# Eight more key rows kept on the chip between two attentions, and a second operand moved from PSUM to SBUF

## The chip, the core and the metric

The kernel runs on one core of a Trainium2 chip. The core has five engines with queues of their own: TensorE (PE, matrix products, here into PSUM), VectorE (DVE), ScalarE (ACT), GpSimd (POOL) and SyncE (SP, which here only issues transfers). Two memories are on the core, SBUF and PSUM, each with 128 partitions; the inputs lie in HBM and come into SBUF by DMA. The metric is the device time of one launch in microseconds (us), the median of some runs.

## What is computed

Two transformer layers' worth of decoding for one new token in a batch of two, in float32, with the weights of the one layer used twice:

```python
def _A_ref(x, k_cache, v_cache, wq, wo):
    B, Sq, D = x.shape            # 2, 1, 576
    H, Dh = 32, 128               # caches: [2, 32, 8192, 128]
    q = (x @ wq).reshape(B, Sq, H, Dh).transpose(0, 2, 1, 3)
    scores = jnp.einsum("bhqd,bhkd->bhqk", q, k_cache) * (Dh ** -0.5)
    p = _softmax(scores, axis=-1)
    o = jnp.einsum("bhqk,bhkd->bhqd", p, v_cache)
    return o.transpose(0, 2, 1, 3).reshape(B, Sq, H * Dh) @ wo
...
x = A_x
x = x + _A_ref(_layernorm(x), A_k_cache, A_v_cache, A_wq, A_wo)
x = x + _B_ref(_layernorm(x), B_w_gate, B_w_up, B_w_down)
x = x + _A_ref(_layernorm(x), A_k_cache, A_v_cache, A_wq, A_wo)
x = x + _B_ref(_layernorm(x), B_w_gate, B_w_up, B_w_down)
```

`_B_ref` is a gated feed-forward block (576 to 4608 and back, gelu times the second product). Each cache holds 2 x 32 x 8192 x 128 floats, 268 MB, and each attention reads both of them: that is nearly all of the traffic.

## The kernel before

**Items.** A head's keys lie over the partitions by rows. Item 0 to 59 are pairs of heads of one batch element (64 partitions to a head, 128 key rows to a partition, 8 parts of 16 rows, 8.39 MB for keys and as much for values); items 60 to 63 (`SINGLE`) are single heads (128 partitions, 64 rows, 4 parts of 16 rows, 4.19 MB). The first attention (layer 0) goes through items 0 to 63, the second (layer 1) from 63 down to 0.

**Held data.** SBUF is filled by one arena, the tile `space`. At the end of the first attention the keys of items 62 and 63 and the values of 61 to 63 stay where they are and are used again in the second. Of item 61's keys, part 3 is copied to PSUM (`kept`, line 643) and copied back in the second attention (line 686); its parts 0 to 2 are loaded again.

**Scores of one item.** For each part, `multiply` (line 637) multiplies key rows by q on VectorE (line 651). The broadcast q of an item, `qb[n]`, is a matrix product in the PSUM tile `bank` (`query`, line 591, written at line 599). In items of several parts at once that is all; in the first five items of the second attention (`waited`: 63, 62, 61, 60, 59) VectorE takes 12 of a part's 16 rows and GpSimd the other 4 (line 655). GpSimd reads q from `qs`, an SBUF copy that ScalarE makes once for an item (line 650). Then GpSimd adds the upper half of each product row to the lower (line 668) for 9 rows, ScalarE sums the other 7 rows whole (line 661), and VectorE sums the halved rows (line 671, `add_up`). The first and last part of item 63 (`at_once`) have 11 rows summed on VectorE and no halving on GpSimd. `peak`, `highest` and `softmax` make the weights, `values` (line 800) multiplies them with the value rows on TensorE, `gather`, `context` and `divide` finish the item.

**Order.** The schedule is written by hand: each engine runs its instructions in the order in which the code emits them. The loop over items (line 871) puts `add_up`, `peak`, `softmax` of the item before, `values` of one before that and `query` of the next one between the parts of an item. Accesses of the engines to one PSUM bank are kept in emitted order by waits, also where they touch different columns of it; `bank` holds `xps`, two slots for `qb` and unused columns, `bank2` holds small results (`po`, `smalls`, `share`).

**Transfers.** All loads are issued by SP in one order, planned at build time (`plan_first`, `plan_mlp`, `plan_second`). A load is issued once its place in `space` has been given back by the last reader (`done`). In the second attention the order is: q weights; keys of 61 (parts 0, 1, 2) and of 60; keys of 59 and values of 60 part by part, into places of the items that are being used up; keys of 58 in two halves; values of 59 in two halves; then keys 57, values 58, keys 56, values 57 and so on, 8.39 MB each.

**Places used by the change.** `same` (line 461) is a constant [128, 128] matrix for the layer norms; `osb` (line 812) a [128, 128] tile for `gather`; `S` (line 640) holds an item's scores; `prz` (line 444) four slots of softmax weights, of which `idle_products` (line 531) also reads the first 256 columns as something to multiply; `qs` shares its buffer with the layer norm's `xc`.

Of the kernel before, what the change touches and what calls it, by code (L numbers as in the profile page):

```python
# [15 lines left out]
P = 128  # L16
B = 2
# [24 lines left out]
RING = 5 * SLOT  # L42
END = RING + NPLACE * PLACE
HELD = 5
FOLD = 2


# [76 lines left out]
def decode_layers(ctx, tc, x_in, kc, vc, wq, wo, wg, wu, wd, out):  # L124
# [32 lines left out]
    def part_at(at, n):  # L157
        return space[:, at:at + n]
# [1 line left out]
    def part(at):  # L160
        return part_at(at, PART).rearrange("p (j d) -> p j d", d=DH)

    def load(at, n, src, lo, hi):

        t = part_at(at, (hi - lo) * PART).rearrange("p (j d) -> p j d", d=DH)
        nc.sync.dma_start(t, ITEMS[n].source(src)[:, lo * JC:hi * JC, :])

    def cache(key, src, n, slots=None, pieces=None):

# [25 lines left out]

        queue.append(make)

    def one(key, src, n, k, where):

        def make():  # L200
            at = arena.ring((key, k), PART) if where is None else arena.take((key, k), places[where[0]][where[1]], PART)
            if at is None:
                return False
            load(at, n, src, k, k + 1)
            ready.setdefault(key, {})[k] = part(at)
            return True

        queue.append(make)
# [154 lines left out]
    def plan_second():  # L363

        for k in range(4):
            of_half(1, k)
        half_rows(("wq", 1, NU - 1), wq, single[-1], None)
        for k in range(4):
            of_half(0, k)
        last = PAIRS - 1  # L370
        k63, v63, k62, v62 = ("k", 1, SINGLE[3]), ("v", 1, SINGLE[3]), ("k", 1, SINGLE[2]), ("v", 1, SINGLE[2])

        for k in range(3):
            one(("k", 1, SINGLE[1]), kc, SINGLE[1], k, None)
        for k in range(4):
            one(("k", 1, SINGLE[0]), kc, SINGLE[0], k, (k63, k - 1) if k else None)

        one(("k", 1, last), kc, last, 0, (k63, 3))
        turns = iter(range(1, 5)), iter(range(4))
        for kind in "vvvvkkkk":  # L380
            if kind == "k":
                k = next(turns[0])
                one(("k", 1, last), kc, last, k, (k62, k - 1))
            else:
                k = next(turns[1])
                one(("v", 1, SINGLE[0]), vc, SINGLE[0], k, (v63, k))
        for k in range(5, 8):
            one(("k", 1, last), kc, last, k, (v62, k - 5))
        half(("k", 1, last - 1), kc, last - 1, 0, 5)
        half(("k", 1, last - 1), kc, last - 1, 4, 4)  # L390
        half(("v", 1, last), vc, last, 0, 0)
        half(("v", 1, last), vc, last, 4, 1)
        for n in range(last - 2, -1, -1):
            cache(("k", 1, n), kc, n)
            cache(("v", 1, n + 1), vc, n + 1)
        cache(("v", 1, 0), vc, 0, None, (4, 2, 1, 1))
        for g in groups(1):
            out_rows(1, g)
# [56 lines left out]
    for i in range(2):  # L455
# [2 lines left out]
    strip = consts.tile([P, 4], F32, name="strip")  # L458
    nc.vector.reduce_sum(strip, ident.rearrange("p (c r) -> p c r", c=4), axis=AX.X)

    same = consts.tile([P, P], F32, name="same")
    nc.vector.tensor_copy(
        same.rearrange("p (m b) -> p m b", b=B), pick[:, 0:B].unsqueeze(1).to_broadcast([P, P // B, B])
    )

# [16 lines left out]
    share = bank2[:, 2 * GH + 2 * P:2 * GH + 2 * P + FOLD * JC]  # L484
    kept = psum1.tile([P, JC, DH], F32, name="kept")

    def small(p, n):

        smalls.append(smalls.pop(0))
        return smalls[0][0:p, 0:n]  # L490


    def norm(split=False, then=None):
        stats = work.tile([P, 6], F32, name="stats")
        nc.vector.bn_stats(stats, x)
        apart = work.tile([P, 4, 6], F32, name="apart")
        nc.vector.tensor_mul(
            apart, stats.unsqueeze(1).to_broadcast([P, 4, 6]), strip.unsqueeze(2).to_broadcast([P, 4, 6])
        )
        every4 = small(P, 4 * 6)  # L500
        nc.tensor.matmul(every4, same, apart.rearrange("p c t -> p (c t)"), start=True, stop=True)
        mv = work.tile([P, 2], F32, name="mv")
        nc.vector.bn_aggr(mv, every4)
        xc = once.tile([P, CW, 2], F32, name="xc", tag="xc")
        xr = x.rearrange("p (m r) -> p r m", r=NU)
        xs = xc.rearrange("p w s -> p (w s)")
        if split:
            xm = xs[:, :5 * 32].rearrange("p (u m e) -> p u m e", u=5, e=2)
            parts = [(xm[:, 0:4, :, e], xr[:, 5 * e:5 * e + 4, :], 0) for e in range(2)]
            parts += [(xm[:, 4, :, e], xr[:, 4, :], e) for e in range(2)]  # L510
            xs = xs[:, :5 * 32].rearrange("p (u q) -> p u q", u=5)
        else:
            parts = [(xc[:, :, s], x, s) for s in range(2)]
            xs = xs.rearrange("p (q u) -> p u q", u=NU)
        for to, of_x, s in parts:
            nc.vector.tensor_scalar(to, of_x, mv[:, 0:1], side[:, s:s + 1], op0=ALU.subtract, op1=ALU.mult)
        u = xs.shape[1]
        nc.vector.transpose(xt[:, PAD:PAD + 32 * u].rearrange("p (u q) -> p u q", u=u), xs)
        if then is not None:
            then()  # L520
        ve = work.tile([P, 1], F32, name="ve")
        nc.vector.tensor_scalar_add(ve, mv[:, 1:2], EPS)  # L522
        rstd = work.tile([P, 1], F32, name="rstd")
        nc.gpsimd.tensor_tensor(out=rstd, in0=ve, in1=mhalf, op=ALU.pow)  # L524
        return rstd
# [22 lines left out]
    def attention(layer):  # L548
# [75 lines left out]
        def own_rows(n, k, m):  # L624

            return 11 if at_once(n, k) else 9 if waited(n) else m * JC

        def keys(n, k, m):

            key = name("k", layer, n)  # L630
            if m == 1:
                return ready[key][k]
            return part_at(arena.live[key, k][0], m * PART).rearrange("p (j d) -> p j d", d=DH)

        qs = once.tile([P, 2, DH], F32, name="qs", tag="xc")

        def multiply(n, k, m):

            if k == 0:
                S[n] = work.tile([P, SK * 2 // P], F32, name="S")  # L640
            u = t = keys(n, k, m)
            if n == SINGLE[1] and k == 3 and layer == 0:
                nc.scalar.copy(kept, t)
            if layer == 0 and n in KEYS_HELD:
                u = ready["products"][k % 2]
            every = m * JC
            rows = 12 if waited(n) else every
            q = qs[:, n % 2, :]
            if rows < JC and k == 0:
                nc.scalar.copy(q, qb[n])  # L650
            nc.vector.tensor_tensor(  # L651
                out=u[:, :rows, :], in0=t[:, :rows, :], in1=qb[n].unsqueeze(1).to_broadcast([P, rows, DH]), op=ALU.mult
            )
            if rows < JC:
                nc.gpsimd.tensor_tensor(
                    out=u[:, rows:, :], in0=t[:, rows:, :], in1=q.unsqueeze(1).to_broadcast([P, JC - rows, DH]),
                    op=ALU.mult,
                )
            r = own_rows(n, k, m)
            for j in range(r, every):  # L660
                nc.scalar.activation(  # L661
                    u[:, j, :], u[:, j, :], AF.Copy, accum_out=S[n][:, k * JC + j:k * JC + j + 1]
                )
            if at_once(n, k):
                prod[n, k] = u[:, :r, :]
                return
            half = prod[n, k] = u[:, :r, :DH // 2]
            nc.gpsimd.tensor_tensor(out=half, in0=half, in1=u[:, :r, DH // 2:], op=ALU.add)  # L668
# [140 lines left out]

        def gather(n):  # L810

            t = osb[n] = work.tile([P, DH], F32, name="osb")
            q = accumulator(n).rearrange("p (r d) -> p r d", r=4)
            nc.vector.tensor_tensor(out=q, in0=q, in1=diag.unsqueeze(2).to_broadcast([P, 4, DH]), op=ALU.mult)  # L814
            nc.vector.tensor_reduce(out=t, in_=q.rearrange("p r d -> p d r"), axis=AX.X, op=ALU.add)  # L815
# [124 lines left out]
        highest(n)  # L940
        softmax(n)
        if layer == 0:
            project(first)
        total(n)
        inverse(n)
        finish(seq[-3] if layer == 0 else p)
        if layer == 0:
            project(second)

            third, fourth, fifth = groups(layer)[2:5]  # L950
            values(N - 1, 0, 2)
            for g in (third, fourth):
                project(g)
                idle_products(1)
            for k in range(2, ITEMS[n].parts, 2):
                values(N - 1, k, k + 2)
                idle_products(1)
            gather(n)
            project(fifth)
            idle_products(1)  # L960
            context(n)
            divide(n)
        else:
            values(N - 1)
            finish(n)
        for g in groups(layer)[5:] if layer == 0 else groups(layer):
            project(g)
            if layer == 0 and g != groups(layer)[-1]:
# [120 lines left out]
```

## Time and profile before

| | |
|---|---|
| median of 3 runs | 2686.34 us (2686.34 to 2686.61) |
| the profiled execution, its own time | 2686.49 us |
| its span, first to last instruction | 2684.7 us |
| bytes read from HBM | 1153.18 MB |
| VectorE busy | 2028.0 us (76%) |
| GpSimd busy | 1551.4 us (58%) |
| TensorE busy | 916.5 us (34%) |
| ScalarE busy | 163.8 us (6%) |

Times within the trace count from the span's start. The second attention begins at about 1369 us (layer norm), its first key product at 1383 us. In rows of a timeline the first number is the start, the second the length (of several merged instructions together), the bracket the time that the engine stood idle before it and what ended that. In rows by line and shape come the count, the busy time, the mean length of one in ns, and the idle time before. In rows by stretch come, for each engine, busy us and count, then granted TensorE clock, busy share of the 16 DMA engines and GB/s.

### The profile page before, as it was taken

The page shows a single profiled execution, that of the slowest core. Times are in us where ns is not written, and L with a number is a line of the kernel's source. Part 1 is how long each engine was busy: PE and PEld are TensorE (multiplying, and loading weights), DVE is VectorE, ACT ScalarE, POOL GpSimd, SP SyncE. Part 2 cuts the span into 40 slices and gives each one's busy share as a digit, 9 for nine tenths or more (in the row PEclk, how much of TensorE's full clock was granted, in tenths as well). Part 3 has the DMA queues.
Part 4 walks back from the last instruction along what each step waited for, and adds up shares of the span by engine and source line. Part 5 has one row for each costly group of instructions (what it writes and reads, how often), then busy time and mean ns, then how long its engine had stood idle before and what let it go on. Part 6 is the DMA issues. An engine that isn't in the chain of part 4 may idle for free. (4 is left out here: it accounts for less than half of the span.)

```text
span 2684.7 us, 16125 instructions
## 1 busy us (share of the span) xinstructions
PE 916.5 (34%) x6478; PEld 290.0 (11%) x6478; DVE 2028.0 (76%) x973; ACT 163.8 (6%) x786; POOL 1551.4 (58%) x405
## 2 busy tenths in 40 slices
PE   1323332232233233334563333223323323332355
PEld 0100000000001000111221101001000100010022
DVE  4878888888888888867038878888888888888740
ACT  0000000000000000000026000000000000000000
POOL 2546676667666766744028457666766676676520
PEclk7666655665566566566986665566566556655668
DMA  9999999999999999999999999999999999999998
GB/s 422 436 436 425 437 434 434 431 432 435 433 433 432 436 431 433 435 427 426 418 413 434 433 431 436 434 432 431 435 435 431 435 432 433 433 436 429 432 424 375
DMA packets 33947, 1154.23 MB, mean 430 GB/s; under 512 B 4152, under 2 KB 4176, under 8 KB 5968
## 3 DMA queue, kind: packets, MB, share of 16 engines
q1 hardware_dynamic: 33832, 1153.19, 99.8%
q8 instruction: 51, 0.84, 0.1%
q14 instruction: 24, 0.20, 0.0%
q10 hardware_dynamic: 40, 0.01, 0.0%
HBM read 1153.18 MB, written 0.00 MB: 430 GB/s over the span
## 5 line engine op out<-in xcount | busy, mean ns | idle before, releaser
L668 POOL TENSOR_TENSOR space<-space 128x3072 f32<-128x3072 f32 (+3 forms) x221 | 1128.1, 5104 | 487.7 <-DVE space L651 349.8
L651 DVE TENSOR_TENSOR space<-space,bank 128x6144 f32<-128x6144 f32 (+3 forms) x223 | 1112.7, 4990 | 312.9 <-DMA space<-in_A_k_cache_dram 249.6
L671 DVE TENSOR_REDUCE S<-space 128x48 f32<-128x3072 f32 (+3 forms) x223 | 569.3, 2553 | 89.4 <-POOL space L668 89.1
L774 POOL TENSOR_TENSOR space<-space 128x2048 f32<-128x2048 f32 x144 | 390.1, 2709 | 385.6 <-DVE space L771 370.2
L800 PE MATMUL acc<-space,prz 128*8 128x512 f32 x3328 | 510.1, 776 | 201.7 <-DMA space<-in_A_v_cache_dram 197.7
L599 PE MATMUL bank<-qsb,pick 4*64 4x128 f32 (+1 forms) x256 | 46.3, 436 | 857.2 <-DVE space L651 847.1
L771 DVE TENSOR_TENSOR space<-space,bank 128x4096 f32<-128x4096 f32 x48 | 212.2, 4420 | 1.6
L800 PEld LDWEIGHTS acc<-space,prz 128*8 128x8 f32 x3328 | 99.6, 107 | 553.9 <-issue 345.1
L720 ACT ACTIVATE nbs<-bank 128x2 f32<-128x2 f32 (+1 forms) x68 | 11.6, 171 | 1846.2 <-PE bank L705 1799.8
L822 PE MATMUL bank<-of,osb 128*32 128x2 f32 x512 | 40.9, 202 | 237.9 <-DVE osb L815 237.9
L599 PEld LDWEIGHTS bank<-qsb,pick 4*64 4x64 f32 (+1 forms) x256 | 20.6, 200 | 878.7 <-DVE space L651 859.3
L697 PE MATMUL bank<-ident,m 128*1 128x128 f32 x68 | 21.5, 317 | 246.2 <-DVE m L695 246.1
L524 POOL TENSOR_TENSOR rstd<-ve,mhalf 128x1 f32<-128x1 f32 x4 | 2.2, 550 | 168.8 <-DVE ve L522 168.8
L779 PE MATMUL acc<-space,owner 128*8 128x512 f32 x96 | 89.9, 1039 | 0.0
L1020 DVE STREAM_TRANSPOSE o<-o 128x288 f32<-128x288 f32 x4 | 2.8, 689 | 92.4 <-ACT o L1018 92.4
L822 PEld LDWEIGHTS bank<-of,osb 128*32 128x32 f32 x512 | 35.8, 154 | 326.2 <-DVE osb L815 324.9
L736 PE MATMUL bank<-sums,unit 128*128 128x2 f32 x120 | 35.3, 363 | 87.0 <-ACT prz L728 87.0
L814 DVE TENSOR_TENSOR acc<-acc,diag 128x512 f32<-128x512 f32 x64 | 43.5, 679 | 22.9 <-PE acc L800 22.9
L841 ACT ACTIVATE oT<-bank,rinv 32x8 f32<-32x8 f32 x110 | 28.6, 260 | 381.4 <-PE bank L822 380.8
L728 ACT ACTIVATE prz<-S,nbs 64x128 f32<-64x128 f32 (+1 forms) x128 | 50.7, 396 | 17.3 <-POOL prz L718 14.4
L528 DVE TENSOR_TENSOR x<-bank,x 128x144 f32<-128x144 f32 x4 | 1.2, 308 | 65.3 <-PE bank L1046 42.6
L661 ACT ACTIVATE space<-space 128x128 f32<-128x128 f32 x164 | 48.3, 296 | 23.6 <-DVE space L651 21.5
(80 smaller groups left out, 551.5 us busy)
## 6 DMA issues: line engine op xcount, KB each, us to landing
space<-in_A_v_cache_dram SPq DMA_DIRECT2D x8, 4096.0 KB
space<-in_A_k_cache_dram SPq DMA_DIRECT2D x6, 4096.0 KB
space<-in_A_wo_dram SPq DMA_DIRECT2D x15, 1152.0 KB
space<-in_A_k_cache_dram SPq DMA_DIRECT2D x15, 1024.0 KB
space<-in_B_w_down_dram SPq DMA_DIRECT2D x9, 1152.0 KB
space<-in_B_w_gate_dram SPq DMA_DIRECT2D x3, 3456.0 KB
space<-in_A_v_cache_dram SPq DMA_DIRECT2D x10, 1024.0 KB
space<-in_A_wq_dram SPq DMA_DIRECT2D x3, 3072.0 KB
```

The costliest lines, as they stand in the source:

```text
L599: nc.tensor.matmul(qb[n][to, :], pick[32 * c:32 * c + 4, r:r + 1].to_broadcast([4, P // it.heads]), qsb[32 * c:32 * c + 4, (h % 4) * DH:(h ...
L651: nc.vector.tensor_tensor(out=u[:, :rows, :], in0=t[:, :rows, :], in1=qb[n].unsqueeze(1).to_broadcast([P, rows, DH]), op=ALU.mult)
L661: nc.scalar.activation(u[:, j, :], u[:, j, :], AF.Copy, accum_out=S[n][:, k * JC + j:k * JC + j + 1])
L668: nc.gpsimd.tensor_tensor(out=half, in0=half, in1=u[:, :r, DH // 2:], op=ALU.add)
L671: nc.vector.tensor_reduce(out=S[n][:, k * JC:k * JC + own_rows(n, k, m)], in_=prod.pop((n, k)), axis=AX.X, op=ALU.add)
L728: nc.scalar.activation(pr[at, lo:].rearrange("p (g e) -> p g e", e=4)[:, 0:it.rows // 2:2, :], s[at, :it.rows].rearrange("p (g r) -> p g r ...
L771: nc.vector.tensor_tensor(out=t, in0=t, in1=share.unsqueeze(2).to_broadcast([P, rows, DH]), op=ALU.mult)
L774: nc.gpsimd.tensor_tensor(out=t[:, :rows], in0=t[:, :rows], in1=t[:, rows:2 * rows], op=ALU.add)
L779: nc.tensor.matmul(accumulator(n)[0:8, :], owner.rearrange("p a e -> p (a e)"), part_at(arena.live[key, lo][0], 4 * DH), start=False, stop ...
L800: nc.tensor.matmul(accumulator(n)[32 * c:32 * c + 8, :], pr[:, at:at + 8], t[g // 4][:, g % 4 * 4:g % 4 * 4 + 4, :].rearrange("p j d -> p ...
L814: nc.vector.tensor_tensor(out=q, in0=q, in1=diag.unsqueeze(2).to_broadcast([P, 4, DH]), op=ALU.mult)
L822: nc.tensor.matmul(po[lo:lo + 32, i, :], t[:, i::GH], of, start=True, stop=True)
```

## The change

**Eight rows more.** Of part 2 of item 61's keys the second attention loads only the first 8 of 16 rows (`less`). The other 8 rows are copied by ScalarE in the first attention: row 8 and most of row 9 into unused columns of `bank2`, most of row 10 into unused columns of `bank`, ends of rows 9 and 10 into small places, row 11 into the middle of a new tile `scores`, rows 12 and 13 into a new tile `home`, rows 14 and 15 into `qs`, and from there, after the last softmax of the first attention, into `prz`. In the second attention the product of that part is made from there: 8 rows in one VectorE instruction, six small ones for rows 8 to 11, two GpSimd instructions for rows 12 to 15, and a memset that clears `prz` again.

**Room for it.** `S` becomes two halves of `scores` in place of a tile with two buffers; `osb` and `same` become one tile `wide`, and the constant is written into it again (`spread`) after each attention's last `gather`.

**q from SBUF.** In the five items with `rows < JC`, VectorE's product reads q from `qs` in place of `qb[n]` for every part but the first (`by`).

```diff
-    def load(at, n, src, lo, hi):
+    def load(at, n, src, lo, hi, less=0):
+        rows = (hi - lo) * JC - less
+        t = part_at(at, rows * DH).rearrange("p (j d) -> p j d", d=DH)
+        nc.sync.dma_start(t, ITEMS[n].source(src)[:, lo * JC:lo * JC + rows, :])
...
-            one(("k", 1, SINGLE[1]), kc, SINGLE[1], k, None)
+            one(("k", 1, SINGLE[1]), kc, SINGLE[1], k, None, JC - STASH if k == 2 else 0)
...
+    wide = consts.tile([P, P], F32, name="wide")
+    def spread():
+        nc.vector.tensor_copy(
+            wide.rearrange("p (m b) -> p m b", b=B), pick[:, 0:B].unsqueeze(1).to_broadcast([P, P // B, B])
+        )
...
+    scores = consts.tile([P, 2 * P], F32, name="scores")
+    home = consts.tile([P, 2 * DH + 16], F32, name="home")
...
+    low, mid = bank2[:, 2 * GH + 2 * P:], bank[:, CW + 2 * DH:]
+    over = low.shape[1] - DH
+    short = DH - over
+    two = prz[:, 0:2, :].rearrange("p a e -> p (a e)")
+    stash = [
+        (8, 0, DH, low[:, :DH]),
+        (9, 0, over, low[:, DH:]), (9, over, DH, two[:, 2 * DH:2 * DH + short]),
+        (10, 0, mid.shape[1], mid), (10, mid.shape[1], DH, home[:, 2 * DH:]),
+        (11, 0, DH, scores[:, DH // 2:DH // 2 + DH]),
+    ]
+    late_rows = [(12, home[:, :2 * DH]), (14, two[:, :2 * DH])]
...
             if k == 0:
-                S[n] = work.tile([P, SK * 2 // P], F32, name="S")
+                at = slice(seq.index(n) % 2 * P, seq.index(n) % 2 * P + P)
+                if n >= PAIRS:
+                    at = slice(0, P // 2) if at.start == 0 else slice(P + P // 2, 2 * P)
+                S[n] = scores[:, at]
             u = t = keys(n, k, m)
+            if n == SINGLE[1] and k == 0 and layer == 0:
+                rest = ready[key_of(n)][2].rearrange("p j d -> p (j d)")
+                for r, lo, hi, to in stash:
+                    if to.shape[1] == short:
+                        to = qs[:, 2 * DH:]
+                    nc.scalar.copy(to, rest[:, r * DH + lo:r * DH + hi])
+                for (r, _), to in zip(late_rows, (home, qs)):
+                    nc.scalar.copy(to[:, :2 * DH], rest[:, r * DH:(r + 2) * DH])
...
+            by = q if rows < JC and k else qb[n]
+            kept_rows = layer == 1 and n == SINGLE[1] and k == 2
+            r = STASH if kept_rows else rows
             nc.vector.tensor_tensor(
-                out=u[:, :rows, :], in0=t[:, :rows, :], in1=qb[n].unsqueeze(1).to_broadcast([P, rows, DH]), op=ALU.mult
+                out=u[:, :r, :], in0=t[:, :r, :], in1=by.unsqueeze(1).to_broadcast([P, r, DH]), op=ALU.mult
             )
-            if rows < JC:
+            if kept_rows:
+                for r, lo, hi, of_row in stash:
+                    nc.vector.tensor_tensor(out=u[:, r, lo:hi], in0=of_row, in1=q[:, lo:hi], op=ALU.mult)
+                for r, of_row in late_rows:
+                    nc.gpsimd.tensor_tensor(
+                        out=u[:, r:r + 2, :], in0=of_row.rearrange("p (j d) -> p j d", d=DH),
+                        in1=q.unsqueeze(1).to_broadcast([P, 2, DH]), op=ALU.mult,
+                    )
+                nc.gpsimd.memset(prz[:, 0:2, :], 0.0)
+            elif rows < JC:
...
-            t = osb[n] = work.tile([P, DH], F32, name="osb")
+            t = osb[n] = wide
...
         softmax(n)
         if layer == 0:
+            nc.scalar.copy(two, qs)
             project(first)
...
             finish(n)
+        spread()
```

More of the change, by code (lines that the diff above doesn't have):

```diff
@@ L44 @@
 HELD = 5
+STASH = 8
 FOLD = 2
@@ L161, in part @@
         return part_at(at, PART).rearrange("p (j d) -> p j d", d=DH)
-    def load(at, n, src, lo, hi):
-        t = part_at(at, (hi - lo) * PART).rearrange("p (j d) -> p j d", d=DH)
-        nc.sync.dma_start(t, ITEMS[n].source(src)[:, lo * JC:hi * JC, :])
+    def load(at, n, src, lo, hi, less=0):
+        rows = (hi - lo) * JC - less
+        t = part_at(at, rows * DH).rearrange("p (j d) -> p j d", d=DH)
+        nc.sync.dma_start(t, ITEMS[n].source(src)[:, lo * JC:lo * JC + rows, :])
     def cache(key, src, n, slots=None, pieces=None):
@@ L196, in half, with one @@
         queue.append(make)
-    def one(key, src, n, k, where):
+    def one(key, src, n, k, where, less=0):
         def make():
@@ L203, in make @@
                 return False
-            load(at, n, src, k, k + 1)
+            load(at, n, src, k, k + 1, less)
             ready.setdefault(key, {})[k] = part(at)
@@ L459, in decode_layers @@
     nc.vector.reduce_sum(strip, ident.rearrange("p (c r) -> p c r", c=4), axis=AX.X)
[L461 to L464, printed above, removed]
+    wide = consts.tile([P, P], F32, name="wide")
[6 more added lines that the diff above has]
+    home = consts.tile([P, 2 * DH + 16], F32, name="home")
     xt = consts.tile([P, PAD + NU * 32], F32, name="xt")
@@ L500, in norm @@
         every4 = small(P, 4 * 6)
-        nc.tensor.matmul(every4, same, apart.rearrange("p c t -> p (c t)"), start=True, stop=True)
+        nc.tensor.matmul(every4, wide, apart.rearrange("p c t -> p (c t)"), start=True, stop=True)
         mv = work.tile([P, 2], F32, name="mv")
@@ L626, in own_rows, with key_of @@
             return 11 if at_once(n, k) else 9 if waited(n) else m * JC
+        def key_of(n):
+            return name("k", layer, n)
         def keys(n, k, m):
-            key = name("k", layer, n)
+            key = key_of(n)
             if m == 1:
@@ L633, in keys @@
             return part_at(arena.live[key, k][0], m * PART).rearrange("p (j d) -> p j d", d=DH)
-        qs = once.tile([P, 2, DH], F32, name="qs", tag="xc")
+        qs = once.tile([P, 2 * DH + short], F32, name="qs", tag="xc")
         def multiply(n, k, m):
             if k == 0:
-                S[n] = work.tile([P, SK * 2 // P], F32, name="S")
+                at = slice(seq.index(n) % 2 * P, seq.index(n) % 2 * P + P)
+                if n >= PAIRS:
+                    at = slice(0, P // 2) if at.start == 0 else slice(P + P // 2, 2 * P)
+                S[n] = scores[:, at]
             u = t = keys(n, k, m)
+            if n == SINGLE[1] and k == 0 and layer == 0:
[6 more added lines that the diff above has]
+                    nc.scalar.copy(to[:, :2 * DH], rest[:, r * DH:(r + 2) * DH])
             if n == SINGLE[1] and k == 3 and layer == 0:
@@ L647, in multiply @@
             rows = 12 if waited(n) else every
-            q = qs[:, n % 2, :]
+            q = qs[:, n % 2 * DH:n % 2 * DH + DH]
             if rows < JC and k == 0:
                 nc.scalar.copy(q, qb[n])
+            by = q if rows < JC and k else qb[n]
+            kept_rows = layer == 1 and n == SINGLE[1] and k == 2
+            r = STASH if kept_rows else rows
             nc.vector.tensor_tensor(
-                out=u[:, :rows, :], in0=t[:, :rows, :], in1=qb[n].unsqueeze(1).to_broadcast([P, rows, DH]), op=ALU.mult
+                out=u[:, :r, :], in0=t[:, :r, :], in1=by.unsqueeze(1).to_broadcast([P, r, DH]), op=ALU.mult
             )
-            if rows < JC:
+            if kept_rows:
[8 more added lines that the diff above has]
+            elif rows < JC:
                 nc.gpsimd.tensor_tensor(
@@ L965, in attention @@
             finish(n)
+        spread()
         for g in groups(layer)[5:] if layer == 0 else groups(layer):
```

## Prediction

> **What bounds the kernel now.** I read the page's header, slices and queue table first, then the stretches around the start of the second attention, because there the change sits.
>
> ```profile
> PE 916.5 (34%) x6478; PEld 290.0 (11%) x6478; DVE 2028.0 (76%) x973; ACT 163.8 (6%) x786; POOL 1551.4 (58%) x405
> DMA  9999999999999999999999999999999999999998
> q1 hardware_dynamic: 33832, 1153.19, 99.8%
> HBM read 1153.18 MB, written 0.00 MB: 430 GB/s over the span
> ```
> ```profile
> 1400.00:1410.00 10.00, 7.11 (x38) 1.88 (x37) 7.78 (x9) 5.97 (x40) 6.12 (x5) 0.62 1.01 419
> 1440.00:1450.00 10.00, 6.89 (x49) 2.59 (x45) 7.99 (x11) 7.11 (x47) 7.96 (x7) 0.67 1.01 436
> ```
>
> The load queue is busy for 99.8% of the span, in every slice. So time has two handles only: fewer bytes, or a load that is issued so late that the queue runs empty; what an engine gains or loses otherwise is not seen. I therefore need the margin of the loads in the stretch that the change touches:
>
> ```profile
> 1432.90 10.39 SPq L166 DMA_DIRECT2D space<-in_A_k_cache_dram  x2
> ...
> 1466.91 0.33 SPq L166 DMA_DIRECT2D space<-in_A_k_cache_dram  x1
> 1488.50 0.33 SPq L166 DMA_DIRECT2D space<-in_A_v_cache_dram  x1
> 1499.99 0.33 SPq L166 DMA_DIRECT2D space<-in_A_k_cache_dram  x1
> ```
> ```profile
> 1499.99 34.44 DMA space<-in_A_k_cache_dram
> ```
>
> The load issued at 1499.99 (keys of 56) landed 34.44 later, at 1534.4. A pair is 8.39 MB, 19.5 us at 430 GB/s, so counted back, values 58 landed at 1514.9, keys 57 at 1495.4, the halves of values 59 at 1475.9 and 1466.1, those of keys 58 at 1456.4 and 1446.6. Values 58, issued at 1488.50, thus came 6.9 us before the load ahead had landed, keys 57 (1466.91) 9.0. The tightest is the second half of keys 58, issued at 1442.96 (1432.90 + 10.39 - 0.33): 3.6, and the queue shows no gap there (share 1.01). So 3.6 is enough, and values 58 may come 3.3 us later before the queue empties, keys 57 5.4 us; keys 58 have a margin near nothing. Beyond that each us late is a us lost, once: the largest lateness counts, not their sum.
>
> **Bytes.** Part 2 of item 61's keys shrinks by 8 rows x 128 partitions x 512 bytes = 0.524 MB: 1.22 us at 430 GB/s. That is all that the change can save.
>
> **The first attention.** ScalarE gets eight copies of 1024 elements together and one of 264.
>
> ```profile
> L643 ACT COPY kept<-space 128x2048 f32<-128x2048 f32 x1 | 1.9, 1857 | 0.0
> L650 ACT COPY qs<-bank 128x128 f32<-128x128 f32 x5 | 1.2, 248 | 0.2 <-PE bank L599 0.2
> ```
>
> Between these two copies a column costs 0.84 ns, so an instruction has 0.14 us fixed: 8 x 0.14 + 1024 x 0.00084 = 2.0 us, and 0.36 for the last. Item 61's first product waits behind the copies into its bank, about 0.9 us. ScalarE is 6% busy, and DVE waits for loads at that place; I cost it at nothing. If that cover were gone it would be 0.9 us. The two `spread` copies, of 128 columns on DVE, lie where DVE waits for the output projections: nothing. `osb` loses its second buffer, but two gathers are an item (two loads of 19.5 us) apart: nothing. The shared halves of `scores` do not overlap in time: nothing.
>
> **The start of the second attention.** These rows carry the rest:
>
> ```profile
> 1382.98 1.75 DVE L651 TENSOR_TENSOR space<-space,bank 128x1536 f32<-128x1536 f32 x1 [11.02 <-ACT qs L650]
> 1384.77 1.62 DVE L671 TENSOR_REDUCE S<-space 128x11 f32<-128x1408 f32 x1
> 1391.94 3.42 DVE L651 TENSOR_TENSOR space<-space,bank 128x1536 f32<-128x1536 f32 x2 [5.56 <-PE bank L599]
> ...
> 1400.86 0.22 DVE L695 TENSOR_REDUCE m<-S 128x1 f32<-128x64 f32 x1
> ...
> 1403.32 3.42 DVE L651 TENSOR_TENSOR space<-space,bank 128x1536 f32<-128x1536 f32 x2 [1.50 <-ACT qs L650]
> ...
> 1414.48 1.75 DVE L651 TENSOR_TENSOR space<-space,bank 128x1536 f32<-128x1536 f32 x1 [1.85 <-ACT qs L650]
> ...
> 1427.65 1.75 DVE L651 TENSOR_TENSOR space<-space,bank 128x1536 f32<-128x1536 f32 x1 [1.84 <-ACT qs L650]
> ...
> 1441.56 1.75 DVE L651 TENSOR_TENSOR space<-space,bank 128x1536 f32<-128x1536 f32 x1 [1.70 <-ACT qs L650]
> ...
> 1461.77 4.41 DVE L651 TENSOR_TENSOR space<-space,bank 128x4096 f32<-128x4096 f32 x1
> ```
> ```profile
> 1391.42 0.48 PE L599 MATMUL bank<-qsb,pick 4*128 4x128 f32 x2
> ```
>
> *What it removes.* Item 63's second product waits 5.56 us for a product into `bank` that makes the next item's q, stuck on PE behind the q weights; its own q was there at 1382.98. With q in SBUF that wait is gone: it can start at 1384.77 + 1.62 = 1386.4. Everything after it in the stretch may move up by some 5.5 us.
>
> *What it adds.* VectorE's product then has both operands in SBUF while GpSimd reads SBUF too. No row of this trace shows that pair side by side: the large products that overlap GpSimd have one operand in PSUM, as the rows above and below say, and the one small exception is the last:
>
> ```profile
> L651 DVE TENSOR_TENSOR space<-space,bank 128x2048 f32<-128x2048 f32 x24 | 54.7, 2280 | 27.7 <-DMA space<-in_A_k_cache_dram 22.9 <-issue 3.9 <-PE bank L599 0.7
> L651 DVE TENSOR_TENSOR space<-space,bank 128x1536 f32<-128x1536 f32 x24 | 41.8, 1747 | 23.8 <-ACT qs L650 17.9 <-PE bank L599 5.6 <-ACT space L686 0.3
> L668 POOL TENSOR_TENSOR space<-space 128x576 f32<-128x576 f32 x22 | 30.9, 1406 | 13.4 <-DVE space L651 13.4
> L655 POOL TENSOR_TENSOR space<-space,qs 128x512 f32<-128x512 f32 x24 | 30.4, 1270 | 17.4 <-ACT qs L650 16.9 <-ACT space L686 0.5
> L671 DVE TENSOR_REDUCE S<-space 128x9 f32<-128x576 f32 x22 | 16.4, 746 | 0.6 <-POOL space L668 0.5
> L671 DVE TENSOR_REDUCE S<-space 128x11 f32<-128x1408 f32 x2 | 3.2, 1614 | 0.0
> L661 ACT ACTIVATE space<-space 128x128 f32<-128x128 f32 x164 | 48.3, 296 | 23.6 <-DVE space L651 21.5 <-POOL space L655 2.0
> L933 DVE SCALAR_TENSOR_TENSOR qsb<-acc,rstd,qsb 128x512 f32<-128x512 f32 x1 | 0.7, 742 | 0.0
> L766 DVE TENSOR_TENSOR bank<-prz 128x32 f32<-128x32 f32 x48 | 9.6, 200 | 24.0 <-PE bank L697 24.0
> ```
>
> L766 reads two SBUF operands, but is only 0.2 us long. So the price is bounded: nothing if both run side by side as now, and if they shut each other out the sum of their times. A part then takes 1.75 (L651) + 1.41 (L668) + 1.27 (L655) = 4.42 us in place of GpSimd's own 2.68. I take the upper end. The nearest row is GpSimd's own: from 512 to 576 elements it pays 2.1 ns an element, VectorE with one SBUF operand 1.04 (1747 to 2280 ns for 512 more). An engine that takes two operands from SBUF at twice the time of one looks as if read paths were scarce, and a third and fourth stream would have to come through them.
>
> The Trainium skill ("SBUF — State Buffer", "Who interferes with whom") has a rule against this change: a VectorE instruction with two SBUF inputs takes the read port that GpSimd uses, and whichever starts first holds it for its whole instruction. By it the sum is the upper end; no run here shows it yet.
>
> Item by item with that end, in emitted order:
> - 63: products 2 and 3 from 1386.4 back to back (3.49), halving (1.41), GpSimd's product (1.27), product 4 (1.75), halving (1.41), then sums 0.75, L933 0.74, sums 1.61: 1398.8 in place of 1400.86. **-2.0.**
> - 62: product, product, then halving, GpSimd, product twice over, halving, GpSimd, and ScalarE's last four sums and the q copy (4 x 0.29 + 0.25) ahead of the next item: 4 x 1.75 + 3 x 1.41 + 3 x 1.27 + 1.41 = 16.4, in place of 11.16 (1403.32 to 1414.48). **+5.3.**
> - 61: 16.4, and its split part: 4 rows less by 1.04 ns a column saves 0.53, six pieces of 512 columns together cost 0.53 and six fixed times of 0.15 (L766: 0.200 less 32 columns), so +0.9; two GpSimd halves of 0.73 in place of one 1.27, +0.2. 17.5 in place of 13.17. **+4.4.**
> - 60: 16.4 in place of 13.91. **+2.5.**
> - 59, eight parts: two products and six rounds of 4.42 (30.0), a halving and its sums (2.15): 32.2 in place of 20.21. **+12.0.**
>
> Sum at the end of 59: +22.2. Keys 57 would be 22.2 - 5.4 = 16.8 us late, values 58, which need item 59's softmax, 22.2 - 3.3 = **18.9**: the queue stands still that long. The saved 1.22 us lies inside this, as the restart is set by the engines. After it nothing is lost: the chain waits 34.4 us for keys 56, so the engines have room to catch up. 2686.49 (the profiled execution) + 18.9 = 2705.4; the median stands 0.15 below that execution: **2705.2**.
>
> **Rivals.**
>
> *Side by side.* If two SBUF operands cost GpSimd nothing, the stretch moves up 5.5 us, the split part's 1.1 us is hidden in that, no load is late, and the bytes are earned: 2686.34 - 1.22 = **2685.1**, not slower. For it: the overlap with one SBUF operand is free now (L651 keeps 1747 ns beside GpSimd). It decides at the first halving of item 63: 1.4 us long and beside product 3, or after it.
>
> *Half.* If they share rather than exclude, the lateness lies midway between -5.5 and +22.2, +8.4, less 3.3: +5.1, **2691.4**. For it: nothing excludes partial sharing; against: no row of two engines here stretches by a part.
>
> *GpSimd first.* If GpSimd's next instruction takes its turn ahead of a waiting product each time, VectorE also waits a GpSimd instruction (1.3) at some five item changes: 26 to 29 less 3.3: **2710 to 2712**.
>
> *Extra work eats the bytes.* If the wait on PE stays although q is in SBUF, the split part's 0.9 falls on a load with no margin (keys 58): the queue waits 0.9 more than before and the 1.2 saved as well: **2687**.
>
> **How the numbers follow.** Shut out, VectorE first: 0.60; GpSimd first 0.07; half 0.10; side by side 0.20; extra work 0.03. The likeliest has its own range of 2697 (some rounds hidden by the waits for ScalarE) to 2713. To leave no more than 2 in 10 outside I go down to side by side: 2684.8 to 2713. A change under 0.2% (5.4 us) can't be told from none: side by side, extra work and half of the half case are the same, 0.28 less 0.02 for a larger gain that I don't see; slower 0.72.
>
> **What would show it.** In the changed trace, item 63's second product at 1386.4 without a wait on PE shows the removed wait. Right: L668 of 576 elements or L651 of 1536 recorded longer, or starting only as the other ends; item 59 taking some 32 us; a gap of the queue (share under 1) near 1490 to 1510. Wrong: item 59 at 20 us, a DMA share of 1 throughout and 1152.66 MB: then side by side holds. A loss with the queue full throughout would break the whole frame.

## The result and the profile after

The changed kernel takes 2698.18 us (median of 6 runs, 2697.72 to 2698.54), the kernel before, timed beside it, 2686.35 us (2686.23 to 2686.74): 11.8 us more, a ratio of 1.0044 with a 95% interval of 1.0031 to 1.0057. The forecast was slower, 2705.2 us, with a range of 2684.8 to 2713.

The page after, header and queue table:

```profile
span 2696.7 us, 16149 instructions
PE 915.9 (34%) x6478; PEld 290.2 (11%) x6478; DVE 2035.7 (75%) x981; ACT 167.7 (6%) x795; POOL 1578.7 (59%) x407
...
DMA  9999999999999999999998999999999999999999
q1 hardware_dynamic: 33832, 1152.67, 99.4%
...
HBM read 1152.66 MB, written 0.00 MB: 427 GB/s over the span
```

Half a megabyte less is read, and yet the span is 12.0 us longer; the queue's share falls from 99.8% to 99.4%, and one slice falls below 9 tenths. Stretches of the changed kernel around it (the last two columns are the DMA share and GB/s):

```profile
1420.00:1430.00 10.00, 6.17 (x36) 1.93 (x36) 8.38 (x14) 7.92 (x41) 9.94 (x7) 0.57 0.90 357
1430.00:1440.00 10.00, 1.71 (x12) 0.85 (x8) 7.67 (x8) 6.48 (x42) 9.30 (x6) 0.77 0.79 297
...
1470.00:1480.00 10.00, 0.00 (x0) 0.00 (x0) 7.42 (x5) 5.81 (x36) 9.79 (x6) 0.50 0.88 374
1480.00:1490.00 10.00, 1.64 (x7) 0.86 (x7) 7.79 (x5) 0.17 (x1) 6.68 (x2) 0.50 0.79 315
...
1500.00:1510.00 10.00, 5.33 (x48) 2.02 (x40) 9.97 (x5) 0.00 (x0) 5.28 (x2) 0.98 0.78 315
```

Three holes: 1420 to 1440 (keys 59 and 58 late), 1470 to 1490 (keys 57), 1500 to 1510 (values 58). What is short of 1 in these five rows sums to 1.0 + 2.1 + 1.2 + 2.1 + 2.2 = 8.6 us; 1 to 3 hundredths missing in the other stretches up to 1560 make most of the rest.

The loads that close the last two holes, from the timeline of the changed kernel's SP:

```profile
1483.05 0.33 SPq L168 DMA_DIRECT2D space<-in_A_k_cache_dram  x1
1505.37 0.33 SPq L168 DMA_DIRECT2D space<-in_A_v_cache_dram  x1
```

Keys 57 are issued 16.1 us later than before (1466.91), values 58 16.9 later (1488.50).

Where the engines lost it, in the groups by line and shape of the changed kernel (count, busy us, mean ns of one, then the idle time before):

```profile
L716 POOL TENSOR_TENSOR space<-space 128x576 f32<-128x576 f32 x22 | 51.2, 2326 | 4.7 <-DVE space L690 4.7
L690 DVE TENSOR_TENSOR space<-space,qs 128x1536 f32<-128x1536 f32 x18 | 36.5, 2032 | 0.0
L703 POOL TENSOR_TENSOR space<-space,qs 128x512 f32<-128x512 f32 x23 | 35.2, 1532 | 15.3 <-ACT qs L686 15.3
L690 DVE TENSOR_TENSOR space<-space,bank 128x1536 f32<-128x1536 f32 x5 | 8.8, 1754 | 18.3 <-ACT qs L686 18.3
```

L716, L690 and L703 are the lines 668, 651 and 655 of before. The five products that still read q from PSUM take 1.75 us as before, the 18 with q in SBUF 2.03, GpSimd's halving 2.33 in place of 1.41. The waiting is recorded as length, not as idle time. One after the other they look like this (timelines of DVE and of POOL in the changed kernel, item 59):

```profile
1456.76 0.75 DVE L719 TENSOR_REDUCE scores<-space 128x9 f32<-128x576 f32 x1 [1.10 <-POOL space L716]
1457.42 2.14 DVE L690 TENSOR_TENSOR space<-space,qs 128x1536 f32<-128x1536 f32 x1
1460.86 0.75 DVE L719 TENSOR_REDUCE scores<-space 128x9 f32<-128x576 f32 x1 [1.30 <-POOL space L716]
1461.53 2.13 DVE L690 TENSOR_TENSOR space<-space,qs 128x1536 f32<-128x1536 f32 x1
```
```profile
1456.68 1.26 POOL L703 TENSOR_TENSOR space<-space,qs 128x512 f32<-128x512 f32 x1
1457.91 2.92 POOL L716 TENSOR_TENSOR space<-space 128x576 f32<-128x576 f32 x1
1460.79 1.26 POOL L703 TENSOR_TENSOR space<-space,qs 128x512 f32<-128x512 f32 x1
```

VectorE's product is issued at 1457.42 while GpSimd's product (L703) runs to 1457.94; it ends at 1459.56, which is 1.6 after that. The halving is issued at 1457.91 and lasts 2.92, of which 1.27 remain after the product's end. So they take turns, the waiting product ahead of GpSimd's next instruction, and a round (a part's product, halving and GpSimd product) takes 4.1 us (1457.42 to 1461.53).

### The profile page after: what moved, and what is told of

The parts are those of the page before. It is cut to its first block, busy times and chain, and to the rows that moved or that the text cites. A ratio compares the mean times of both kernels' runs of the same rounds, so it can differ in the third digit from the quotient of the medians.

```text
span 2696.7 us, 16149 instructions
## 1 busy us (share of the span) xinstructions
PE 915.9 (34%) x6478; PEld 290.2 (11%) x6478; DVE 2035.7 (75%) x981; ACT 167.7 (6%) x795; POOL 1578.7 (59%) x407
## 3 DMA queue, kind: packets, MB, share of 16 engines
q1 hardware_dynamic: 33832, 1152.67, 99.4%
## 5 line engine op out<-in xcount | busy, mean ns | idle before, releaser
L716 POOL TENSOR_TENSOR space<-space 128x3072 f32<-128x3072 f32 (+3 forms) x221 | 1148.6, 5197 | 474.0 <-DVE space L690 340.6
L690 DVE TENSOR_TENSOR space<-space,bank 128x6144 f32<-128x6144 f32 (+3 forms) x204 | 1079.8, 5293 | 302.9 <-DMA space<-in_A_k_cache_dram 230.5
L719 DVE TENSOR_REDUCE scores<-space 128x48 f32<-128x3072 f32 (+3 forms) x223 | 569.4, 2553 | 104.2 <-POOL space L716 104.0
L822 POOL TENSOR_TENSOR space<-space 128x2048 f32<-128x2048 f32 x144 | 390.3, 2710 | 385.9 <-DVE space L819 370.5
L870 PE MATMUL bank<-of,wide 128*32 128x2 f32 x512 | 40.8, 201 | 237.9 <-DVE wide L863 237.9
L870 PEld LDWEIGHTS bank<-of,wide 128*32 128x32 f32 x512 | 35.8, 154 | 326.0 <-DVE wide L863 324.8
L776 ACT ACTIVATE prz<-scores,nbs 64x128 f32<-64x128 f32 (+1 forms) x128 | 50.7, 396 | 17.2 <-POOL prz L766 14.4
```

What stands on the lines that cost most here:

```text
L690: nc.vector.tensor_tensor(out=u[:, :r, :], in0=t[:, :r, :], in1=by.unsqueeze(1).to_broadcast([P, r, DH]), op=ALU.mult)
L719: nc.vector.tensor_reduce(out=S[n][:, k * JC:k * JC + own_rows(n, k, m)], in_=prod.pop((n, k)), axis=AX.X, op=ALU.add)
L776: nc.scalar.activation(pr[at, lo:].rearrange("p (g e) -> p g e", e=4)[:, 0:it.rows // 2:2, :], s[at, :it.rows].rearrange("p (g r) -> p g r ...
L822: nc.gpsimd.tensor_tensor(out=t[:, :rows], in0=t[:, :rows], in1=t[:, rows:2 * rows], op=ALU.add)
L870: nc.tensor.matmul(po[lo:lo + 32, i, :], t[:, i::GH], of, start=True, stop=True)
```

## Experiments

The theory: the loss is VectorE's products with two SBUF operands and GpSimd's SBUF-reading instructions shutting each other out, and the loads that come late for it. Rivals: the eight kept rows cost by themselves; the loss is not a matter of late loads. Times are medians; the kernel before, timed beside these runs, took 2686.33 us (2686.03 to 2686.76, 27 runs) in the first four and 2686.38 in the last three.

**q back in PSUM, the kept rows stay.**

```diff
-            by = q if rows < JC and k else qb[n]
+            by = qb[n]
```

> The changed kernel with q from PSUM again in every part (the eight kept rows stay). Exclusion theory (VectorE products with both operands in SBUF and GpSimd instructions that read SBUF run one after the other): the loss goes, items 62, 61, 60, 59 take 11.2, about 14, 13.9, 20.2 us again, 2685.5 to 2687. Rival (the eight rows cost by themselves: copies, six small pieces, waits on their PSUM banks): stays near 2698, at least above 2692.

2685.96 us (2685.38 to 2686.71, 11 runs; ratio 0.9999, 0.9991 to 1.0008). The loss is gone with the one operand, and the kept rows cause none of it. First products of items 61, 60 and 58 in its timeline:

```profile
1414.47 1.75 DVE L690 TENSOR_TENSOR space<-space,bank 128x1536 f32<-128x1536 f32 x1 [1.85 <-ACT qs L686]
...
1427.64 1.75 DVE L690 TENSOR_TENSOR space<-space,bank 128x1536 f32<-128x1536 f32 x1 [1.84 <-ACT qs L686]
...
1461.77 4.41 DVE L690 TENSOR_TENSOR space<-space,bank 128x4096 f32<-128x4096 f32 x1
```

They are those of before to 0.01 us, item 61 with its split part included: it takes 13.17 us as without it. ScalarE sets its length: the product that follows waits 1.84 us for ScalarE's copy of q, in both kernels. The bytes alone earn 0.4 of the 1.2 us by the medians, which is not clear of the noise: the runs of the two kernels overlap.

**q from SBUF, without the kept rows** (the kernel before, with the line `by` and `qb[n]` replaced by it).

> The kernel before with q from SBUF in the parts after the first of the five items, no kept rows. Exclusion theory: 2697 to 2699, with 1153.18 MB, as the restart of the loads is set by the engines and not by the bytes. Rival (kept rows): 2686.

2698.39 us (2697.71 to 2698.9; ratio 1.0045, 1.0031 to 1.0059), the changed kernel's time with 0.524 MB more to read. The move of q is the whole loss, and the bytes saved are lost in it: the engines set the restart (values 58 are issued at 1505.16 here and at 1505.37 in the changed kernel).

**The wait removed in another way.** Item 63's second product waited for item 62's q product in `bank`. Here q stays in PSUM and that product is emitted after item 63's last part.

```diff
-                if j == 0 and not last and not first:
+                if j == (3 if layer == 1 and i == 0 else 0) and not last and not first:
```

> The changed kernel with q from PSUM, and item 62's q product emitted after item 63's last part in place of its first, so that item 63's other parts don't wait for it. Exclusion theory with a load queue that only loses when a load is late: item 63's second product at 1386.4, no load late, the 0.524 MB are earned: 2685.0 to 2685.3. Rival (the kept rows can't be earned): 2686.3 or more.

2685.19 us (2685.01 to 2685.38, 11 runs). Its ratio, 0.9996 (0.9987 to 1.0005), does not leave 1 by its interval, but none of its runs lies within the runs of before (2686.03 at the least). 1.14 of the 1.22 us are earned. Its timeline:

```profile
1386.16 3.41 DVE L690 TENSOR_TENSOR space<-space,bank 128x1536 f32<-128x1536 f32 x2
...
1456.00 4.41 DVE L690 TENSOR_TENSOR space<-space,bank 128x4096 f32<-128x4096 f32 x1
```

Item 63's second product starts at 1386.2 without a wait, and item 58 5.8 us earlier than before. It is the fastest version but for the one below that ties with it.

**The same without kept rows.**

> The kernel before with the late q product alone. If time is bytes and late loads only: engines 5 us ahead, nothing earned, 2686.2 to 2686.4. Rival (the engines' lead is worth time by itself): up to 5 us less, 2681 to 2685.

2686.48 us (2686.07 to 2686.95; ratio 1.0, 0.9992 to 1.0009). The engines are 5.6 us ahead (item 58's first product at 1456.13) and nothing is earned: here, with a full queue, only bytes and late loads count.

**q from SBUF in one item only.** Item 63, then item 59:

```diff
-            by = q if rows < JC and k else qb[n]
+            by = q if n == N - 1 and rows < JC and k else qb[n]
...
+            by = q if n == PAIRS - 1 and rows < JC and k else qb[n]
```

> The changed kernel with q from SBUF in item 63 alone (three products). Exclusion theory: these three run one after the other with GpSimd, but item 63's wait is gone too; its peak near 1398.4 in place of 1400.9, the later items as long as before the change, no load late: 2685.0 to 2685.5. Rival (any use of the SBUF copy costs): above 2687.

> The changed kernel with q from SBUF in item 59 alone (seven products). Exclusion theory: item 59 takes about 30.2 us in place of 20.2, values 58 are some 10.9 us late with the kept rows' 0.9, the margin there is about 4 us: 2692 to 2694. If the loss were the sum over all parts rather than the largest lateness, 7 of 19 parts of 11.8 us: 2690.5 with the bytes. Rival (loss sits in the early items): 2686.

Item 63 alone: 2685.16 us (2684.9 to 2685.62). Its peak comes at 1397.97, between 1400.86 (before) and 1395.09 (the late q product): the three products with q in SBUF cost some 2.9 us, paid by the removed wait. No load is late.

Item 59 alone: 2692.46 us (2692.23 to 2692.93; ratio 1.0022, 1.0013 to 1.0032), within the 2692 to 2694 expected. From its timelines and stretches:

```profile
1441.61 1.75 DVE L690 TENSOR_TENSOR space<-space,bank 128x1536 f32<-128x1536 f32 x1 [1.71 <-ACT qs L686]
...
1471.79 4.41 DVE L690 TENSOR_TENSOR space<-space,bank 128x4096 f32<-128x4096 f32 x1
```
```profile
1499.57 0.33 SPq L168 DMA_DIRECT2D space<-in_A_v_cache_dram  x1
```
```profile
1470.00:1480.00 10.00, 1.06 (x5) 0.37 (x5) 8.78 (x5) 2.12 (x14) 7.34 (x4) 0.50 0.73 285
1490.00:1500.00 10.00, 9.52 (x71) 3.92 (x69) 9.97 (x5) 0.00 (x0) 3.68 (x1) 0.76 0.73 315
```

Item 59 takes 30.18 us in place of 20.21, values 58 are issued 11.1 us late, and the kernel loses 6.1, which is 5.0 less. The changed kernel's values 58 were 16.9 late and it lost 11.8, 5.0 less too; without the kept rows it is 16.7 and 12.1, 4.6 less. So the loss is the lateness of this load, less an amount that is nearly the same each time; a sum over parts would have given 2690.5.

That amount is not the margin alone. Once the queue is full again, the loads of these kernels are issued later than before by a steady time. The issue of one load (keys of 53) in the kernel before, the changed kernel and this one:

```profile
1623.62 0.33 SPq L166 DMA_DIRECT2D space<-in_A_k_cache_dram  x1
```
```profile
1636.88 0.33 SPq L168 DMA_DIRECT2D space<-in_A_k_cache_dram  x1
```
```profile
1631.12 0.33 SPq L168 DMA_DIRECT2D space<-in_A_k_cache_dram  x1
```

The lag is 13.3 and 7.5 us, so that the margin is 16.9 - 13.3 = 3.6 and 11.1 - 7.5 = 3.6 (without the kept rows 16.7 - 13.2 = 3.5). Near 2400 us the lag has shrunk to 12.05 and 6.4. In between, single distances from one load to the next are longer than their like, and not at the same places in every kernel (in the kernel before 21.6 in place of 20.3 us, from 2378.90 to 2400.52); what causes them is not shown.

**GpSimd that only writes.** In the five items, its products and halvings become two memsets each of the same places; the scores of these rows are left out of this kernel.

```diff
-                nc.gpsimd.tensor_tensor(
-                    out=u[:, rows:, :], in0=t[:, rows:, :], in1=q.unsqueeze(1).to_broadcast([P, JC - rows, DH]),
-                    op=ALU.mult,
-                )
+                for _ in range(2):
+                    nc.gpsimd.memset(u[:, rows:, :], 0.0)
...
+            if rows < JC:
+                for _ in range(2):
+                    nc.gpsimd.memset(half, 0.0)
+                return
```

> The changed kernel, with GpSimd's products and halvings in the five items replaced by two memsets of the same places each (those scores are left out). If VectorE's second operand is shut out by GpSimd's reads alone: products of 1536 columns stay at 1.75 us beside the memsets, no load late, about 2685.1. If any GpSimd access to SBUF shuts it out: products or memsets longer, items of 59's kind above 21 us, 2687 or more.

2685.51 us (2685.17 to 2685.76; ratio 0.9996, 0.9987 to 1.0006). Its groups by line and shape:

```profile
L690 DVE TENSOR_TENSOR space<-space,qs 128x1536 f32<-128x1536 f32 x18 | 31.4, 1749 | 0.1
L716 POOL MEMSET space<- 128x576 f32 x44 | 25.4, 577 | 31.3 <-DVE space L690 29.8
L704 POOL MEMSET space<- 128x512 f32 x46 | 24.0, 524 | 1.3
L697 POOL TENSOR_TENSOR space<-home,qs 128x256 f32<-128x256 f32 x1 | 1.3, 1329 | 0.0
```

The same 18 products with q in SBUF are back at 1.75 us beside a GpSimd that writes SBUF and, but for the two small products of the kept rows (L697), reads none. One of these two shows the rule from the other side: issued while VectorE's product of 1024 columns with q in SBUF runs, it is recorded at 1329 ns, where it takes 737 with q in PSUM. The memsets are not stretched either: two memsets of 132 and 264 columns in this kernel take 210 and 320 ns, 0.83 ns a column, by which 512 columns give 0.53 us. So it is GpSimd's reading that shuts out the second operand, which is what the Trainium skill says ("SBUF — State Buffer", "Who interferes with whom": two SBUF inputs contend with a GpSimd instruction that reads SBUF, not with one that only writes). Every GpSimd product and halving here reads two operands; one that reads a single operand was not run.

## Why the prediction was right, and where its sizes were off

The way and the mechanism were right; the size was not: 18.9 us were forecast and 11.8 measured. That the time lies in the range says little, as the range reached from the rival "side by side" to the full sum.

**The frame** (time is bytes and late loads) held: 5.6 us of engine lead earn nothing, 0.524 MB earn 1.14 us where no load is late.

**The removed wait** held: item 63's second product starts at 1386.51 without a wait, predicted 1386.4.

```profile
1386.51 3.42 DVE L690 TENSOR_TENSOR space<-space,qs 128x1536 f32<-128x1536 f32 x2
```
```profile
1388.33 2.85 POOL L716 TENSOR_TENSOR space<-space 128x576 f32<-128x576 f32 x1 [2.60 <-DVE space L690]
```

**The exclusion** held as a mechanism, at the place that the prediction named: the first halving of item 63 (the second row) is recorded at 2.85 us, and the pair of products ends at 1389.93, 1.25 us before it does. In its turn each takes about its usual time: 1.6 and 1.27 us in the rows of item 59 above. The choice of the upper bound was right, and "side by side" and "half" fell. "GpSimd first" fell as well: in the rows above the waiting product goes ahead of GpSimd's next instruction (its sum, 26 to 29 less 3.3, would have been 2709 to 2712, not 2710). "Extra work eats the bytes" fell with the wait on PE gone and item 61's 13.17 us.

**The lateness was mis-sized: 22.2 predicted, 16.1 measured at the end of item 59** (its successor's first product at 1477.91 in place of 1461.77). Item 63's peak and the first products of the items after it in the changed kernel:

```profile
1398.36 0.22 DVE L743 TENSOR_REDUCE m<-scores 128x1 f32<-128x64 f32 x1
...
1400.82 1.75 DVE L690 TENSOR_TENSOR space<-space,bank 128x1536 f32<-128x1536 f32 x1 [1.50 <-ACT qs L686]
...
1416.42 1.75 DVE L690 TENSOR_TENSOR space<-space,bank 128x1536 f32<-128x1536 f32 x1 [1.85 <-ACT qs L686]
...
1432.05 1.75 DVE L690 TENSOR_TENSOR space<-space,bank 128x1536 f32<-128x1536 f32 x1 [1.93 <-ACT qs L686]
...
1447.73 1.75 DVE L690 TENSOR_TENSOR space<-space,bank 128x1536 f32<-128x1536 f32 x1 [1.97 <-ACT qs L686]
...
1477.91 4.41 DVE L690 TENSOR_TENSOR space<-space,bank 128x4096 f32<-128x4096 f32 x1
```

| item | predicted change | measured |
|---|---|---|
| 63, to its peak | -2.0 | 1398.36 - 1400.86 = -2.5 |
| 62 | +5.3 | 15.60 - 11.16 = +4.4 |
| 61 | +4.4 | 15.63 - 13.17 = +2.5 |
| 60 | +2.5 | 15.68 - 13.91 = +1.8 |
| 59 | +12.0 | 30.18 - 20.21 = +10.0 |

Two terms did it. A round was summed from recorded lengths, 1.75 + 1.41 + 1.27 = 4.42; but in the rows above successive instructions overlap at their ends, and a round takes 4.10: item 59's last five rounds take 20.49 us (1457.42 to 1477.91) in place of 22.10, 1.6 of the 2.0 us by which that item was forecast too long. And item 61's split part, +1.1, costs next to nothing: the distance from its product (1422.05) to the next (1426.31) is 4.26 us, against 4.10 for a whole part, and items 60 and 62 are as long as 61. Values 58 then come 16.9 late and not 16.1, because TensorE's 61 products with value rows ahead of that load take 8.97 us in place of 8.23.

**The margin held, and "after it nothing is lost" missed a gain:** 3.3 predicted, 3.6 measured once the queue is full again. It is then 13.3 us behind, where 18.9 was predicted: 5.3 of the difference is the lateness of values 58 (22.2 and 16.9), 0.3 the margin. The whole kernel loses 11.8; the other 1.4 come back later, and the cause of that is open.

**ScalarE's copies** held: eight copies take 2.27 us by their rows (2.0 predicted), and the second attention's first product comes at 1383.18 in place of 1382.98.

**Left open:** why the kept rows alone earn 0.4 and not 1.2 us. Keys 58, whose issue times there are those of before, had no margin by the prediction, but the trace shows the queue full at that place. It falls short earlier: in the stretches 1404 to 1408 and 1408 to 1412 that kernel moves 385 and 320 GB/s, the kernel before 422 and 416, the one with the late q product 424 and 422. That is 0.53 MB, as much as the kept rows save; a likely reading is that the loads there, issued when they were before, can't come earlier until the engines do. How it still earns 0.4, and how that varies by 1.3 us from run to run, is not shown.

## What to carry to other kernels

Before an operand is moved out of PSUM, ask what reads SBUF beside that instruction: two engines that each keep pace can become one. Where a queue bounds the time, price an edit by the lateness of the next load less its margin, and measure the margin with one run that is late by a known amount, at the loads that follow it and not by the whole time alone. A false wait on a shared bank can be removed by moving the instruction waited for, which here costs nothing, in place of moving the operand.

## What was not expected of the hardware

Being shut out shows in no wait of the instruction that is shut out: GpSimd's halving is recorded at 2326 ns in place of 1406 and its busy total rises from 1551.4 to 1578.7 us. A length that grows with the same shape is the sign. Short instructions grow most in proportion. The split part's pieces of 8 and 16 columns, both operands in SBUF, in the kernel with q in PSUM and in the changed kernel:

```profile
L695 DVE TENSOR_TENSOR space<-prz,qs 128x8 f32<-128x8 f32 x1 | 0.2, 213 | 0.0
L695 DVE TENSOR_TENSOR space<-home,qs 128x16 f32<-128x16 f32 x1 | 0.2, 158 | 0.0
```
```profile
L695 DVE TENSOR_TENSOR space<-home,qs 128x16 f32<-128x16 f32 x1 | 0.6, 585 | 0.0
L695 DVE TENSOR_TENSOR space<-prz,qs 128x8 f32<-128x8 f32 x1 | 0.6, 576 | 0.0
```

And there was nothing to win in the operand's place itself: a product of 1536 columns takes 1749 ns with q in SBUF and GpSimd only writing, 1747 with q in PSUM.
